# Seven block products for eight in the second matmul of a fused attention and feed-forward kernel

## The chip, the cores and the metric

The kernel runs on one core of a Trainium2 chip. The core has five engines that run side by side, each with its own instruction queue: TensorE (PE in the profile; its weight loads stand apart as PEld), VectorE (DVE), ScalarE (ACT), GpSimd (POOL) and SyncE (SP), which here only issues DMAs. Matmul results land in PSUM, which has eight banks of 128 partitions x 512 float32. The metric is the device time of one execution in microseconds (us), the median of several.

## The reference

Attention over 32 memory slots per head, then a feed-forward block whose activation is h times cos(h):

```python
a = exp(phi - max(phi, axis=2)); a = a / (sum(a, axis=2) + 1e-09)
k_m, v_m = einsum('bhsm,bhsd->bhmd', a, k), einsum('bhsm,bhsd->bhmd', a, v)
scores = matmul(q, k_m.T) / sqrt(64)
attn = softmax(scores)                 # over the 32 slots
x = matmul(attn, v_m)                  # [4608 tokens, 512]
h = x @ w_in                           # w_in  [512, 2048]
g = h * cos(h)
out = g @ w_out                        # w_out [2048, 512]
```

There are 8 batches, 8 heads, 576 tokens per batch, head width 64, all float32.

## The kernel before, in words

**Work.** The 4608 tokens are cut into 12 groups of 384 (three tiles of 128; GT). d_ff is cut into 16 tiles of 128 (NF). The main loop runs 12 x 16 = 192 iterations (i, L652); iteration i belongs to group grp = i // 16 and tile f = i % 16. v_m is folded into w_in per batch (`fold`, L442: vw), so the first product, `gemm1` (L479), multiplies the folded weights with the attention weights aT and leaves h, transposed, in one PSUM bank hp (128 x 384). Groups 1, 4, 7 and 10 straddle two batches and do this in two halves of 192 columns.

**Precision.** From group 1 on, each float32 factor is held as two float16 parts, and each product is three matmuls: high x high, high x low, low x high.

**Activation.** `act` (L498): ACT scales hp to turns and adds a quarter (L502, u), DVE rounds to int32 (L507) and subtracts (L508). `act_end` (L511): ACT takes the sine (L512), DVE multiplies with hp (L516), ACT rounds to float16 (L518), DVE forms the low part (L519). hp is free after L516.

**Second product.** `gemm2` (L524) runs four iterations later (LAG = 4). For each of the three token tiles it adds three matmuls (g high/low as weights, 512 columns of w_out as the moving side, L537) to that tile's accumulator bank; after f = 15 the banks are scaled out to SBUF (`evacuate`, L544) and stored.

**Banks.** Three for the accumulators, three for hp, two for everything else (`small_ps`).

**Beside it.** While a group runs, the attention of a later batch is made in small steps: `memory` (L214) takes the maximum of phi, its exponential, then k_m and v_m by 80 matmul records per batch over five chunks of kv into one bank psA (L247); for batches 0 to 3 the maximum comes from a transposed copy phiT by DVE and PE, for 4 to 7 by DVE and GpSimd (`maximum`, L204). `attend` (L325) makes scores, exponentials and aT. The lists `jobs` and `folds` (L641 to L649) say in which iterations the steps of a batch are emitted. In group 1 w_out and w_in are split into parts (L660 to L662).

**Order.** The program is written as one list. A scheduler places each engine's instructions in an order of its own, by priority from the place in that list and its own estimates of cost, and hands out buffers on the way; only instructions marked `keep_in_program_order` are bound. On the chip each engine then follows its list strictly and waits where an input is late.

Of the kernel before, what the change touches and what calls it, by code (L numbers as in the profile page):

```python
# [12 lines left out]
I32 = mybir.dt.int32  # L13
# [26 lines left out]
NT = 4  # L40
LAG = 4
# [3 lines left out]
def attention_then_ffn(ctx: ExitStack, tc: tile.TileContext, phi, phiT, kv, qT, w_in, w_out, eye, out):  # L45
# [5 lines left out]
    ps_acc = ctx.enter_context(tc.tile_pool(name="ps_acc", bufs=3, space=PSUM))  # L51
    ps_h = ctx.enter_context(tc.tile_pool(name="ps_h", bufs=3, space=PSUM))
    ps_s = ctx.enter_context(tc.tile_pool(name="ps_s", bufs=2, space=PSUM))

    def small_ps(name):
        return ps_s.tile([P, 512], F32, tag="ps_s", name=name)
# [15 lines left out]

    vl = const.tile([P, NP, 2, M], F16, name="vl")
    nc.vector.memset(vl, 0.0)

    loads, st = {}, {}

    def load_phi(b):
        if b < NT:
            loads["phiT", b] = t = ld.tile([P, 2, S], F32, tag="phiT", name=f"phiT_{b}", bufs=1)  # L80
            nc.sync.dma_start(out=t, in_=phiT[b].rearrange("(g p) s -> p g s", p=P))
# [5 lines left out]
    def load_kv(b):  # L87
        ts = []
        for c, (s0, n) in enumerate(TCH):
            t = ld.tile([P, H * KV], F32, tag="kv", name=f"kv_{b}_{c}", bufs=5)  # L90
            nc.sync.dma_start(out=t[:n], in_=kv[b, s0:s0 + n])
            ts.append(t)
        loads["kv", b] = ts
# [55 lines left out]

    def power_of_two(dst, src):  # L150
# [4 lines left out]
    def to_range(name, pool, tag, e):  # L155
        t = pool.tile([P, 1], F32, tag=tag, name=name)
        nc.vector.reciprocal(out=t, in_=e)
        nc.vector.tensor_scalar(out=t, in0=t, scalar1=2.0 ** 14, scalar2=None, op0=ALU.mult)
        return t

    def weight_scale(kind, name):
# [11 lines left out]
        st["s", name] = to_range(f"s_{name}", const, f"s_{name}", e)  # L173
# [30 lines left out]
    def maximum(b):  # L204
        a = loads["phi", b]
        mx = ld.tile([P, 3, HM], F32, tag="phiT", name=f"mx_{b}", bufs=1)
        nc.vector.tensor_tensor(out=mx[:, 0:2], in0=a[:, 0:2], in1=a[:, 2:4], op=ALU.max)
        nc.vector.tensor_tensor(out=mx[:, 0], in0=mx[:, 0], in1=mx[:, 1], op=ALU.max)
        nc.vector.tensor_tensor(out=mx[0:S - 512, 0], in0=mx[0:S - 512, 0], in1=a[0:S - 512, 4], op=ALU.max)
        nc.gpsimd.partition_all_reduce(mx[:, 2], mx[:, 0], channels=P, reduce_op=RED.max)  # L210
        st["top", b] = mx[:, 2]


    def memory(b):  # L214
        a = loads.pop(("phi", b))
        if b < NT:

            nmx = wk.tile([P, 2], F32, tag="nmx", name=f"nmx_{b}", bufs=1)
            nc.vector.tensor_reduce(out=nmx, in_=loads.pop(("phiT", b)), op=ALU.max, axis=AX.X)
            top = small_ps(f"top_{b}")[:, 0:HM]  # L220
            for g in range(2):
                nc.tensor.matmul(top[:, g * P:(g + 1) * P], lhsT=nmx[:, g:g + 1].broadcast_to([P, P]), rhs=ident,
                                 start=True, stop=True)
        else:
            top = st["top", b]
        yield
        if b >= NT:
            yield
            yield
        for c0, c1, n in ((0, 2, P), (2, 4, P), (4, 5, S - 512)) if b == 0 else ((0, 4, P), (4, 5, S - 512)):  # L230
            ins = nc.vector.tensor_tensor(out=a[:n, c0:c1], in0=a[:n, c0:c1],
                                          in1=top[:n].unsqueeze(1).broadcast_to([n, c1 - c0, HM]),
                                          op=ALU.subtract)
            if b >= NT:

                tc.keep_in_program_order(ins)
# [4 lines left out]
        kvs = loads.pop(("kv", b))  # L241
        psA = small_ps(f"psA_{b}")
# [496 lines left out]
```

## Time and profile before

| what | value |
|---|---|
| median of 3 runs | 720.79 us (718.35 to 721.98) |
| the profiled execution | 718.65 us, its span 716.6 us |
| TensorE clock granted | 0.99 of full speed |
| PE busy | 694.8 us, 97% |
| DVE busy | 570.0 us, 80% |
| ACT busy | 520.8 us, 73% |
| POOL busy | 14.1 us, 2% |
| groups 3 to 10 (first products start at 226.0 and 656.3 us) | 430.3 us |

The span runs from the first to the last instruction; the profiled execution's own time is 2.05 us longer. Matmuls are pipelined: one is booked from its start to its modelled end, so that neighbours overlap, and the time from one start to the next is shorter than the duration booked. Where consecutive instructions of a group are merged into a row "x9", the row's time in the chain of waits is the time that the nine took out of the span.

### The profile page before, as it was taken

To read this page: it belongs to the slowest core of one execution; us is meant where nothing else is said; L and a number is where in the kernel's file an instruction comes from. 1 tells how busy PE (TensorE), PEld (TensorE's weight loads), DVE (VectorE), ACT (ScalarE), POOL (GpSimd) and SP (SyncE) were. 2 spreads that over 40 slices of the span, in tenths; PEclk is the share of its full clock that TensorE was granted. 3 is DMA by queue.
4 is the path that set the end of the run, shared out by engine and by line. 5 is a ranking of instruction groups with operands and counts; after the bars stand their busy time and mean duration, and the time that the engine had idled before them with its cause. 6 is when DMAs were issued, how large, how long until landed. Compare 5 with 4: busy or idle time off the path is not lost.

```text
span 716.6 us, 12018 instructions
## 1 busy us (share of the span) xinstructions
PE 694.8 (97%) x4578; PEld 357.2 (50%) x4578; DVE 570.0 (80%) x1256; ACT 520.8 (73%) x965; POOL 14.1 (2%) x34
## 2 busy tenths in 40 slices
PE   7689999999999999999999999999999999999997
PEld 3244444565454445565444544666444544555553
DVE  2868999998988997679877997679776987676753
ACT  1789999899886875668757685678767785665653
POOL 0000000000000000000000100000000000000000
PEclk9799999999999999999999999999999999999999
DMA  8995881426405300152103310152100000100101
GB/s 291 381 330 168 310 291 42 121 60 188 149 7 161 111 1 1 45 167 67 45 1 123 107 49 1 45 167 68 44 1 1 22 24 1 45 1 1 45 0 45
DMA packets 31561, 66.78 MB, mean 93 GB/s; under 512 B 2192, under 2 KB 11024, under 8 KB 31504
## 3 DMA queue, kind: packets, MB, share of 16 engines
q1 hardware_dynamic: 27184, 58.15, 25.1%
q10 hardware_dynamic: 4320, 7.87, 2.9%
q8 instruction: 36, 0.59, 0.3%
q14 instruction: 21, 0.17, 0.1%
HBM read 52.38 MB, written 9.44 MB: 86 GB/s over the span
## 4 chain that ended last, share of the span: by engine, by line
PE 60%; ACT 17%; DVE 16%; DMA 4%; issue 2%; SPq 1%; POOL 0%; ACTq 0%; DVEq 0%
PE acc L537 34%; PE hp L493 18%; PE pv L432 3%; ACT u L512 2%; DVE u L516 2%; DMA phi<-in_phi 2%; DVE u L508 2%; DVE gp L519 2%; ACT u L502 2%; ACT L512 2%; DVE gp L507 1%; DMA kv<-in_kv 1%; PE sc L349 1%; ACT L237 1%; PE psA L247 1%
## 5 line engine op out<-in xcount | busy, mean ns | idle before, releaser
L537 PE MATMUL acc<-wo,gp 128*128 128x512 f16 x1584 | 371.2, 379 | 0.0
L537 PEld LDWEIGHTS <-gp 128*128 128x128 f16 x1584 | 153.4, 98 | 161.5 <-issue 2.6
L493 PE MATMUL hp<-aT,vw 128*128 128x192 f16 (+1 forms) x1440 | 202.6, 284 | 0.8 <-DVE u L516 0.4
L493 PEld LDWEIGHTS <-vw 128*128 128x128 f16 x1440 | 125.1, 98 | 82.3 <-issue 30.0
L512 ACT ACTIVATE u<-u 128x384 f32<-128x384 f32 x192 | 99.7, 522 | 86.6 <-DVE u L508 85.7
L516 DVE SCALAR_TENSOR_TENSOR u<-hp,u 128x384 f32<-128x384 f32 x176 | 96.8, 552 | 45.7 <-ACT u L512 43.4
L502 ACT ACTIVATE u<-hp,cu 128x192 f32<-128x192 f32 (+1 forms) x240 | 110.3, 491 | 18.2 <-PE hp L493 11.8
L519 DVE TENSOR_TENSOR gp<-u,gp 128x384 f16<-128x384 f32 x176 | 96.6, 551 | 29.9 <-ACT gp L518 29.3
L518 ACT CAST gp<-u 128x384 f16<-128x384 f32 x176 | 89.0, 509 | 38.7 <-DVE u L516 36.7
L508 DVE TENSOR_TENSOR u<-u,gp 128x384 f32<-128x384 f32 x192 | 105.7, 552 | 3.2
L507 DVE CAST gp<-u 128x384 int32<-128x384 f32 x192 | 67.4, 353 | 20.6 <-ACT u L502 18.9
L532 PE MATMUL acc<-wo,gp 128*128 128x512 f32 x96 | 45.5, 603 | 1.6 <-DVE gp L514 1.6
L439 DVE SCALAR_TENSOR_TENSOR vw<-pv,vw 128x512 f16<-128x512 f32 x48 | 33.0, 689 | 5.1 <-ACT vw L438 3.8
L438 ACT ACTIVATE vw<-pv 128x512 f16<-128x512 f32 x48 | 28.3, 590 | 7.4 <-PE pv L432 6.5
L484 PE MATMUL hp<-aT,vf 128*128 128x384 f32 x64 | 26.4, 546 | 4.2 <-DVE gp L514 2.0
L512 ACT ACT_TABLE_LOAD x23 | 29.5, 1283 | 0.4
L532 PEld LDWEIGHTS acc<-wo,gp 128*128 128x128 f32 x96 | 17.0, 190 | 20.7 <-issue 14.9
L247 PE MATMUL psA<-kv,phi 128*32 128x129 f32 (+1 forms) x640 | 23.5, 276 | 2.8 <-DMA kv<-in_kv 1.5
L553 ACT ACTIVATE ob<-acc,os 128x512 f32<-128x512 f32 x28 | 18.5, 682 | 8.1 <-PE acc L537 5.2
L247 PEld LDWEIGHTS psA<-kv,phi 128*32 128x32 f32 (+1 forms) x640 | 16.1, 109 | 13.3 <-issue 6.9
L484 PEld LDWEIGHTS hp<-aT,vf 128*128 128x128 f32 x64 | 12.5, 207 | 17.7 <-DVE gp L514 4.6
L349 PE MATMUL sc<-q,km 128*64 128x256 f32 (+3 forms) x192 | 20.6, 343 | 0.0
(126 smaller groups left out, 549.5 us busy)
## 6 DMA issues: line engine op xcount, KB each, us to landing
kv<-in_kv SPq DMA_DIRECT2D x32, 516.0 KB, 5.8
q<-in_qT SPq DMA_DIRECT2D x8, 1152.0 KB, 6.4
raw_out<-in_w_out SPq DMA_DIRECT2D x8, 1024.0 KB, 5.0
out<-ob ACTq DMA_DIRECT2D x30, 256.0 KB, 2.1
raw_in<-in_w_in SPq DMA_DIRECT2D x6, 1024.0 KB, 8.4
phi<-in_phi SPq DMA_DIRECT2D x8, 512.0 KB, 7.2
w_in_sb<-w_in_parts SPq DMA_DIRECT2D x12, 256.0 KB, 4.1
phiT<-in_phiT SPq DMA_DIRECT2D x4, 576.0 KB, 6.4
```

Source lines behind the costliest of these rows:

```text
L247: nc.tensor.matmul(psA[32 * j:32 * (j + 1), g * KV:(g + 1) * KV], lhsT=a[:n, c, h * M:(h + 1) * M], rhs=kvs[c][:n, h * KV:(h + 1) * KV], s ...
L484: nc.tensor.matmul(hp[:, :GT], lhsT=st["vf", q][:, g, fo * P:(fo + 1) * P], rhs=st["aTf"][:, g], start=(g == 0), stop=(g == 1))
L493: nc.tensor.matmul(hp[:, c0:c0 + n], lhsT=vw[:, wi, g, fo * P:(fo + 1) * P], rhs=aT[:, ai, g, c1:c1 + n], start=(k == 0), stop=(k == 5))
L502: ins = nc.scalar.activation(u[:, c0:c0 + n], hp[:, c0:c0 + n], AF.Copy, scale=st["cu", b] if grp else 1.0 / (2.0 * math.pi), bias=0.25)
L507: nc.vector.tensor_copy(out=ni, in_=u)
L508: nc.vector.tensor_tensor(out=u, in0=u, in1=ni, op=ALU.subtract)
L512: nc.scalar.activation(u, u, AF.Sin, scale=TWO_PI_BELOW)
L516: nc.vector.scalar_tensor_tensor(out=u, in0=hp[:, :GT], scalar=2.0 ** -17, in1=u, op0=ALU.mult, op1=ALU.mult)
L518: nc.scalar.copy(gp[:, 0], u)
L519: nc.vector.tensor_tensor(out=gp[:, 1], in0=u, in1=gp[:, 0], op=ALU.subtract)
L532: nc.tensor.matmul(accs[grp][t], lhsT=gp[:, t * P:(t + 1) * P], rhs=wo[:, f + 1], start=(f == 0), stop=(f == NF - 1))
L537: nc.tensor.matmul(accs[grp][t], lhsT=gp[:, gi, t * P:(t + 1) * P], rhs=parts[:, wi], start=(f == 0 and gi == 0 and wi == 0), stop=(f == N ...
```

## The change

In groups 3 to 10 (FIRST7, LAST7), token tiles 0 and 2 of a group and each pair of d_ff tiles (f even, f odd) form a product of 2 x 2 blocks: two token tiles x two d_ff tiles, times two d_ff tiles x two halves of 256 columns of w_out. It is made by seven block products instead of eight. Token tile 1 goes on as before (accumulator X[4]).

- **PE.** Per pair of f: six matmuls of 512 columns and 21 of 256 (`gemm2_7`), for 18 of 512. Four banks hold the seven sums of products, and a fifth tile 1.
- **Sums of g.** Per pair, four subtractions or additions of 128 x 128 float32 on GpSimd, one after the other (`act7`'s U tile, in `act_end7`).
- **Splits into float16** are made per pair, for nine blocks of 128 instead of six, in three ACT copies and three DVE subtractions (`parts7`), one iteration later.
- **Activation, groups 3 to 11.** ACT writes the scaled turns straight to int32, and one DVE instruction multiplies hp and subtracts, in place of L507 and L508; the quarter turn moves into the sine's bias.
- **Combinations of w_out** for the eight pairs are made once, by six GpSimd instructions each, and split by one ACT and one DVE instruction each (`combine`, `combine_end`), emitted at iterations 22 to 55; they are kept in SBUF that has come free.
- **Evacuation** (`evacuate7`): three ACT reads of PSUM, seven DVE additions or subtractions of 128 x 256, two ACT scalings.
- **Banks.** One tag of three ("any"), and a0, a1, a2, x0, x1 with one each. Before group 3, hp takes "any", "any", x0 in turn, and the small tiles "any", x1. From group 3 on a0 to x1 belong to the sums, and hp and all small tiles share the three of "any".
- **Buffers in SBUF.** kv has three buffers for five; chunks 3 and 4 of batches 2 to 7 are loaded in the middle of `memory`, when the first chunks are done. phiT is now used for all batches and loaded at the end of the `attend` before; `maximum` is gone. aT has two buffers for three. km and vm are cleared once, not per batch. From batch 2 on, the all-partition maximum for the scale of v_m is made by PE and DVE instead of GpSimd.
- **Lag.** LAG7 = 3 entries from group 3 on, counted after the pair has been split.

```diff
-    ps_acc = ctx.enter_context(tc.tile_pool(name="ps_acc", bufs=3, space=PSUM))
-    ps_h = ctx.enter_context(tc.tile_pool(name="ps_h", bufs=3, space=PSUM))
-    ps_s = ctx.enter_context(tc.tile_pool(name="ps_s", bufs=2, space=PSUM))
+    ps = ctx.enter_context(tc.tile_pool(name="ps", bufs=1, space=PSUM))
+    homes = {"h": ["any", "any", "x0"], "s": ["any", "x1"]}
+    turn = {"h": 0, "s": 0}
+    def bank(name, tag):
+        return ps.tile([P, 512], F32, tag=tag, name=name, bufs=3 if tag == "any" else 1)
...
+    def load_kv(b, cs=range(3)):
+        ts = loads.setdefault(("kv", b), {})
+        for c in range(5) if b < 2 else cs:
+            s0, n = TCH[c]
+            if b < 2 and c > 2:
+                t = kx[:, c - 3]
+            else:
+                t = ld.tile([P, H * KV], F32, tag="kv", name=f"kv_{b}_{c}", bufs=3)
...
+    def combine(p):
+        x = wd(p + 1).bitcast(F32) if p < 7 else ew.tile([P, 2, DM], F32, tag="U", name="x_7", bufs=2)
+        for i in range(2):
+            parts = wo_parts(2 * p + i)
+            nc.gpsimd.tensor_tensor(out=x[:, i], in0=parts[:, 0], in1=parts[:, 1], op=ALU.add)
+        a, b, c, d = (x[:, i, HW * j:HW * (j + 1)] for i in range(2) for j in range(2))
+        nc.gpsimd.tensor_tensor(out=a, in0=b, in1=a, op=ALU.subtract)
...
+    def combine_end(p, x):
+        t = wd(p)
+        nc.scalar.copy(t[:, 0].rearrange("p (c x) -> p c x", c=2), x)
+        nc.vector.tensor_tensor(out=t[:, 1].rearrange("p (c x) -> p c x", c=2), in0=x,
+                                in1=t[:, 0].rearrange("p (c x) -> p c x", c=2), op=ALU.subtract)
...
+            elif c == 2:
+                load_kv(b, (3, 4))
+                yield
+                yield
...
-        nc.gpsimd.partition_all_reduce(l3, l2, channels=P, reduce_op=RED.max)
+        if b < 2:
+            nc.gpsimd.partition_all_reduce(l3, l2, channels=P, reduce_op=RED.max)
+        else:
+            t = small_ps(f"l_{b}")[:, 0:P]
+            nc.tensor.matmul(t, lhsT=l2.broadcast_to([P, P]), rhs=ident, start=True, stop=True)
+            nc.vector.tensor_reduce(out=l3, in_=t, op=ALU.max, axis=AX.X)
...
+    def act7(grp, f, hp, pin):
+        if f % 2 == 0:
+            st["U"] = ew.tile([P, 9, TB], F32, tag="U", name=f"U_{grp}_{f}", bufs=2)
...
+            ins = nc.scalar.activation(ni[:, c0:c0 + n], hp[:, c0:c0 + n], AF.Copy, scale=st["cu", b], bias=0.25)
...
+            nc.vector.scalar_tensor_tensor(out=u[:, c0:c0 + n], in0=hp[:, c0:c0 + n], scalar=st["cu", b],
+                                           in1=ni[:, c0:c0 + n], op0=ALU.mult, op1=ALU.subtract)
...
+    def act_end7(grp, f, hp, U, u):
+        nc.scalar.activation(u, u, AF.Sin, scale=TWO_PI_BELOW, bias=quarter)
+        nc.vector.scalar_tensor_tensor(out=u, in0=hp[:, :GT], scalar=2.0 ** -19, in1=u, op0=ALU.mult, op1=ALU.mult)
...
+            for o, x, y, op in ((6, 0, 3, ALU.add), (8, 2, 0, ALU.subtract), (7, 6, 2, ALU.subtract),
+                                (0, 5, 7, ALU.subtract)):
+                nc.gpsimd.tensor_tensor(out=U[:, o], in0=U[:, x], in1=U[:, y], op=op)
...
+    def parts7(grp, f, U):
+        G = ew.tile([P, 2, 9, TB], F16, tag="G", name=f"G_{grp}_{f}", bufs=3)
+        for x, n in ((1, 5), (6, 3), (0, 1)) if grp <= LAST7 else ((0, 6),):
+            nc.scalar.copy(G[:, 0, x:x + n], U[:, x:x + n])
+            nc.vector.tensor_tensor(out=G[:, 1, x:x + n], in0=U[:, x:x + n], in1=G[:, 0, x:x + n], op=ALU.subtract)
+        return [(grp, f - 1, G), (grp, f, G)]
...
+    PARTS = ((0, 0), (0, 1), (1, 0))
+    def gemm2_7(grp, f, G):
+        if f == 0:
+            accs[grp] = [bank(f"acc7_{grp}_{i}", t) for i, t in enumerate(("a0", "a1", "a2", "x0", "x1"))]
+        X, p, last = accs[grp], f // 2, f >= NF - 2
+        w0, w1, d = wo_parts(2 * p), wo_parts(2 * p + 1), wd(p)
+        if f % 2 == 0:
+            for w, t in ((w0, 1), (w1, 4)):
+                for gi, wi in PARTS:
+                    nc.tensor.matmul(X[4], lhsT=G[:, gi, t], rhs=w[:, wi], start=(f == 0 and t == 1 and gi + wi == 0),
+                                     stop=(last and t == 4 and gi == 1))
+            todo = ((0, 0, 2, w0, 0),)
+        else:
+            todo = ((0, 1, 5, w1, 0), (3, 0, 3, d, 2), (1, 0, 6, d, 0), (1, 1, 7, d, 3), (2, 0, 8, d, 1),
+                    (2, 1, 0, w1, 1))
+        for x, half, t, w, col in todo:
+            for gi, wi in PARTS:
+                nc.tensor.matmul(X[x][:, HW * half:HW * (half + 1)], lhsT=G[:, gi, t],
+                                 rhs=w[:, wi, HW * col:HW * (col + 1)],
...
+    def evacuate7(grp):
+        X = accs[grp]
+        es = [wk.tile([P, DM], F32, tag="back", name=f"ob_{grp}_{t}", bufs=4) for t in (2, 0, 1)]
+        nc.scalar.activation(es[2], X[4], AF.Copy, scale=row_scale(grp, 1))
+        nc.scalar.copy(es[0], X[0])
+        nc.scalar.copy(es[1], X[1])
...
+    combos = {22: 0, **{33 + 3 * p: 1 + p for p in range(7)}}
...
+        if i == FIRST7 * NF:
+            homes["h"], homes["s"] = ["any"], ["any"]
+        if i in combos:
+            st["x", combos[i]] = combine(combos[i])
+        if i - 4 in combos:
+            combine_end(combos[i - 4], st.pop(("x", combos[i - 4])))
...
+        was = len(ended)
+        while len(begun) > (grp > LAST7):
+            pending.extend(act_end(*begun.pop(0)))
+        if was:
+            pending.extend(parts7(*ended.pop(0)))
+        if len(pending) > (LAG if grp < FIRST7 else LAG7):
             gemm2(*pending.pop(0))
```

More of the change, by code (lines that the diff above doesn't have):

```diff
@@ L201, in w_in_split, with wd @@
         st["w2", q] = w2
[L204 to L211, printed above, removed]
+    def wd(p):
+        if p < 2:
+            return kx.rearrange("p c x -> p (c x)")[:, p * DM * 2:(p + 1) * DM * 2].bitcast(F16).rearrange(
+                "p (w x) -> p w x", w=2)
+        if p in (4, 5):
+            return w_in_sb[:, 2 * (p - 4):2 * (p - 3), 3 * FS:].bitcast(F16)
+        key = "wd", p // 2
+        if key not in st:
+            st[key] = ld.tile([P, 2, 2, 2 * DM], F16, tag="raw1" if p < 4 else "raw2", name=f"wd_{p // 2}")
+        return st[key][:, p % 2]
```

169 lines of the change are left out of this document (105 added, 64 removed).

## Prediction

> **What bounds the kernel now.** I read the page first, then the stretches of the groups, the chain of waits, the grouped instructions, and single tiles. A difference under 0.5% (3.6 us) counts as none: about what a measurement of this kernel can tell from no change.
>
> The page's busy line, then the stretches of groups 1, 2, 3, 4, 6 and 9 and of groups 3 to 10 together (columns: stretch; its length; PE, weight loads, DVE, ACT, POOL busy; clock; DMA):
>
> ```profile
> PE 694.8 (97%) x4578; PEld 357.2 (50%) x4578; DVE 570.0 (80%) x1256; ACT 520.8 (73%) x965; POOL 14.1 (2%) x34
> ...
> 110.20:166.60 56.40, 56.22 (x348) 31.49 (x347) 55.93 (x116) 51.40 (x109) 0.31 (x1) 1.00 0.29 73
> 166.60:226.00 59.40, 58.81 (x458) 29.25 (x457) 51.11 (x123) 50.45 (x83) 0.97 (x3) 1.00 0.47 142
> 226.00:281.40 55.40, 54.97 (x336) 25.57 (x333) 48.98 (x112) 39.57 (x76) 2.04 (x4) 1.00 0.15 45
> 281.40:337.60 56.20, 56.00 (x485) 33.79 (x484) 42.96 (x101) 40.36 (x83) 2.05 (x4) 1.00 0.27 89
> 392.30:444.50 52.20, 52.20 (x304) 25.39 (x301) 46.90 (x111) 37.27 (x71) 3.05 (x4) 1.00 0.17 55
> 555.30:606.10 50.80, 50.80 (x296) 24.48 (x293) 45.36 (x108) 37.52 (x71) 0.66 (x1) 1.00 0.04 17
> 226.00:656.30 430.30, 428.97 (x3024) 224.30 (x3021) 342.29 (x771) 301.58 (x590) 9.54 (x16) 1.00 0.15 49
> ```
>
> In the 430.3 us that the change touches, PE lacks work for 1.3 us. DVE is second, 80% on the mean but 90% in groups 6 and 9 (46.90 of 52.20), and PE does not stop there: DVE at 90% is no limit yet. In group 1 it ran at 99%. So a saving on PE is a saving in time, as long as DVE, ACT and the banks keep up.
>
> **The change on PE.** Is a matmul of half the columns half the time, though it loads weights as often? Two rows of the chain of waits, back to back: 6 matmuls of 512 columns, then 12 of 192 columns (group 4):
>
> ```profile
> 299.18 1.94 PE acc L537 x9
> 301.12 1.00 PE hp L493 x12
> ```
>
> Nine of 512 take 1.94 us, 216 ns each; twelve of 192 take 1.00, 83 ns each, and each has a weight load of its own, which stays hidden. On the line through both, 256 columns cost 83 + 64 x 133/320 = 110 ns. A pair of f falls from 18 x 216 = 3.89 us to 6 x 216 + 21 x 110 = 3.61, by 0.28 to 0.29. There are 8 groups x 8 pairs: **-18.6 us**, 2.3 in each group.
>
> PE also gains work. The prices of all that follows:
>
> ```profile
> L508 DVE TENSOR_TENSOR u<-u,gp 128x384 f32<-128x384 f32 x192 | 105.7, 552 | 3.2
> L512 ACT ACTIVATE u<-u 128x384 f32<-128x384 f32 x192 | 99.7, 522 | 86.6 <-DVE u L508 85.7
> L516 DVE SCALAR_TENSOR_TENSOR u<-hp,u 128x384 f32<-128x384 f32 x176 | 96.8, 552 | 45.7 <-ACT u L512 43.4
> L519 DVE TENSOR_TENSOR gp<-u,gp 128x384 f16<-128x384 f32 x176 | 96.6, 551 | 29.9 <-ACT gp L518 29.3
> L518 ACT CAST gp<-u 128x384 f16<-128x384 f32 x176 | 89.0, 509 | 38.7 <-DVE u L516 36.7
> L507 DVE CAST gp<-u 128x384 int32<-128x384 f32 x192 | 67.4, 353 | 20.6 <-ACT u L502 18.9
> L502 ACT ACTIVATE u<-hp,cu 128x384 f32<-128x384 f32 x112 | 63.8, 576 | 12.6 <-PE hp L493 8.9 <-ACT ob L553 1.7 <-DVE gp L507 0.4
> L378 DVE SCALAR_TENSOR_TENSOR aT<-back,aT 128x512 f16<-128x512 f32 x14 | 9.5, 678 | 0.0
> L377 ACT ACTIVATE aT<-back 128x512 f16<-128x512 f32 x14 | 8.8, 626 | 1.5 <-DVE back L375 1.1
> L237 ACT ACTIVATE phi<-phi 128x1024 f32<-128x1024 f32 x7 | 7.4, 1057 | 0.1
> L231 DVE TENSOR_TENSOR phi<-phi,mx 128x1024 f32<-128x1024 f32 x4 | 4.9, 1218 | 0.0
> L287 POOL PARTITION_ALL_REDUCE l<-l x8 | 4.0, 495 | 348.5 <-DVE l L285 348.5
> L222 PE MATMUL top<-ident,nmx 128*128 128x128 f32 x16 | 2.5, 281 | 0.5 <-DVE nmx L219 0.5
> L271 POOL MEMSET vm<- 128x256 f32 x8 | 2.5, 319 | 80.1 <-PE pv L426 38.7 <-DVE vl L318 38.5 <-DVE om L565 2.9
> L377 ACT ACTIVATE aT<-back 128x128 f16<-128x128 f32 x7 | 2.1, 297 | 0.2 <-DVE back L375 0.2
> L378 DVE SCALAR_TENSOR_TENSOR aT<-back,aT 128x128 f16<-128x128 f32 x7 | 2.0, 284 | 0.2 <-ACT aT L377 0.2
> L208 DVE TENSOR_TENSOR mx<-mx 128x256 f32<-128x256 f32 x4 | 1.6, 412 | 0.0
> ```
>
> The maximum of phi on PE (L222) cost 2.5 us for four batches and now comes for four more: +2.5. The maximum for the scale of v_m is half of it, in six batches: +1.9. Together **+4.4 us**, in groups 2 to 8. Both are durations with overlap, so ceilings; the floor is nothing, and the range uses it. If all else hides, 718.65 - 18.6 + 4.4 is 14.2 us less.
>
> **DVE.** Gone per f are L507, L508 and L519: 353 + 552 + 551 = 1456 ns, 23.3 us per group. New per f is one instruction like L516: 552 ns, 8.8 us per group; in straddling groups two of 192 columns, about 355 each (L378 gives (678-284)/384 = 1.03 ns a column): 11.4. New per pair are three splits of 640, 384 and 128 columns: 551 + 256 x 1.03 = 814, 551 and 284, 1.65 us, or 13.2 per group. The evacuation adds 7 x 412 (L208) = 2.9. Net per group: +1.6, or +4.2 where it straddles. The split of each w_out combination costs 1.22 (L231, same size): four fall into group 2 and three into group 3. What `maximum` gives back, phiT's reduction takes; I count it zero.
>
> So DVE needs, against PE's need: group 3, 48.98 + 1.6 + 3.7 = 54.2 against about 53.1; group 6, 48.5 against 49.9; group 9, 47.0 against 48.5; group 4, 47.2 against some 55. In group 3 DVE becomes the bound: I take 55.0, so 1.9 us of the gain is lost there. In 6 and 9 it works at 97%, more than the 90% that was free: I charge 1 us each. Group 2 goes to 51.11 + 4.9 = 56.0 of 59.4, ACT to 50.45 + 4 x 1.06 (L237) = 54.7; I charge 1 us.
>
> **ACT.** The three copies per pair cost 297 + 509 + 728 (slope (626-297)/384 from L377) = 1.53 us against 2 x 509 before: +4.1 us per group, and the two scalings of the evacuation some 1.3. Group 6 goes to 42.7 of 50: no bound, since the chain turns, subtraction, sine, product is one instruction shorter than before (L507 is gone).
>
> **GpSimd.** No row shows a two-input instruction there. Nearest are L271, 0.32 us for 256 columns written and none read, so some 0.2 for 128 as floor, and the all-reduce with 0.50 as ceiling. I take 0.3, nearer to the memset, which works per element: four sums per pair are 1.2 us of some 5.5; the combinations (48 instructions, at twice the columns or more some 0.6 to 1.2 us each) have four iterations each, some 13 us. `parts7` stands an iteration behind its sums. That cover holds for an iteration, 2.6 us per pair; beyond it ACT's second copy waits with the next iteration's turns queued behind it.
>
> The Trainium skill has a rule against this (SBUF — State Buffer, "Who interferes with whom"): a DVE instruction with two SBUF inputs and a GpSimd instruction that reads SBUF exclude each other, the later blocking wholly. No row here can show it, as GpSimd hardly reads; rival 2 prices it.
>
> **Banks and kv.** hp and all small tiles now share three banks for five. An hp's least life is 1.0 (gemm1) + 576 + 552 + 522 + 552 = 3.2 us, PE's iteration about 2.6, so two banks pass an hp in time if its life stays under 5.2. A row that speaks against it, with the tiles psA and kv:
>
> ```profile
> 404.15 1.15 PE L493 MATMUL hp<-aT,vw 128*128 128x384 f16 x6
> ...
> 407.56 1.15 PE L493 MATMUL hp<-aT,vw 128*128 128x384 f16 x6
> ...
> 413.78 1.02 DVE L516 SCALAR_TENSOR_TENSOR u<-hp,u 128x384 f32<-128x384 f32 x2
> ...
> L247 PE MATMUL psA<-kv,phi x320: 270/273/298, 305.0 to 555.1; 128*32 128x129 f32 x128, 64*32 64x129 f32 x32
> L261 DVE TENSOR_SCALAR X<-psA,den x8: 341/348/351, 312.6 to 557.5; 128x128 f32<-128x128 f32 x8
> ...
> DMA to landing us min/median/max: 3.5/6.1/13.2
> ```
>
> During an attention step two hp live until 414.3 and 414.8, 10.2 and 7.2 us, because DVE and ACT do other work first. psA held a bank from 305.0 to 312.6 in the first batch of this stretch, and will hold it for a kv load more (6.1 median). PE can bridge this with the second product, of which three to five tiles (1.8 us each) lie ready; so the forecast charges nothing, with rival 3 as the other end. On SP's queue the two late kv loads wait for the first chunks' matmuls, with the next batch's phi and kv behind them; these are due a whole attention step later, so I charge nothing. phiT, now loaded when an attention step ends, must land (about 6 us by the kv row, for a similar size) before the next maximum: only batch 3 follows at once, and PE has first and second products meanwhile.
>
> The new evacuation costs PE nothing: X[4] ends at f = 14, X[0] early in f = 15, and the rest are needed two first products later.
>
> The tail is unchanged: group 11 keeps the old product and its last six tiles.
>
> **Sum.** -18.6 + 4.4 + 1.9 + 2 + 1 = -9.3 against the profiled 718.65: 709.3. The median is 2.1 above that execution, so the forecast is **711.5 us**.
>
> **Rivals.**
>
> 1. *All of it hides.* DVE in group 3 hands work to its neighbours, and 97% is no more of a limit than group 1's 99%: 720.8 - 14.2 = 706.5. For it: PE's idle time of 1.3 us in 430. Against: group 1 was DVE's, not PE's.
>
> 2. *DVE is blocked by GpSimd's sums and becomes the bound.* 24 splits per group read two SBUF operands; if two in three wait for one sum of 0.3, that is 4.8 us of DVE per group. Groups 3, 6 and 9 then take 59.0, 53.3 and 51.8, against 55.4, 52.2 and 50.8: +5.7 instead of a gain. The other five keep 5 x 2.3 - 4.0 = 7.5, group 2 loses 1: net -0.8, 720. By the skill's rule that is about what comes out if sums and splits fall together often. It decides once DVE waits over some 1.5 us per group. Against: sums are emitted one iteration ahead of their splits.
>
> 3. *Banks (slower).* While psA waits for its late kv chunks, some 14 us per batch, two banks serve hp; with lives of 7.2 they pass one per 3.6 us, 4 iterations instead of 5.4, a loss of 3.6. Scores and the exponentials' table loads cost about 2.5 more. Five batches (3 to 7) make 30 us: 720.8 - 14.2 + 30 = 736. It decides from lives over 5.2 us, with the stored second products used up. For it: the 10.2 above. Against: DVE and ACT may be handed another order where banks are few.
>
> That 256 columns cost more than half (weight loads as the limit) I give little: the 83 ns row.
>
> **How the numbers follow.** Forecast 0.38, rival 1 0.25, rival 2 0.20, rival 3 0.14, rest 0.03. Low is 702, rival 1 with PE's new work at its floor (720.8 - 18.6); high is 728, past rival 2 and into the first half of rival 3. Faster by over 3.6 us are the forecast and rival 1 with a little of 2: 0.65. Within: most of rival 2 and a mild 3: 0.18. Slower: the rest, 0.17.
>
> **What would show it.** PE: 1344 matmuls of 256 columns at starts 110 ns apart; groups 5, 8 and 10 shorter by about 2 us with PE never idle. DVE: about 54 us busy in group 3, at 97% in 6 and 9. GpSimd: 256 sums near 0.3 us; if splits on DVE come out longer than 814, 551 and 284, rival 2 is at work. PE's weight loads of the first product waiting for DVE's last use of hp would be rival 3. The forecast is wrong if 256 columns cost over 125 ns, or PE idles over 10 us in groups 3 to 10.

## The result

The changed kernel takes 758.6 us (median of four runs, 756.87 to 759.87) against 720.1 for the kernel before on the same chip: 1.053 times as long, 95% interval 1.050 to 1.057. The forecast was 711.5, faster; the time lies far outside its range. Its profiled execution has a span of 757.0 us.

The profile after: the page's busy line, then the stretches of the changed kernel (columns as in the prediction). The seven are: groups 1, 2, 3, 4, 6, 9, each from the first product of its first tile to that of the next group, and groups 3 to 10 together.

```profile
PE 690.2 (91%) x5182; PEld 419.2 (55%) x5182; DVE 631.5 (83%) x1283; ACT 567.6 (75%) x1039; POOL 202.9 (27%) x313
...
116.00:175.70 59.70, 56.28 (x350) 31.83 (x349) 59.53 (x101) 47.23 (x99) 13.41 (x11) 1.00 0.27 67
175.70:253.40 77.70, 64.94 (x458) 32.22 (x457) 70.77 (x136) 55.79 (x93) 33.31 (x32) 0.91 0.39 118
253.40:310.50 57.10, 53.37 (x375) 29.43 (x372) 51.76 (x103) 44.40 (x82) 24.33 (x35) 1.00 0.16 54
310.50:367.60 57.10, 54.64 (x564) 41.45 (x562) 49.55 (x119) 46.63 (x94) 15.83 (x31) 1.00 0.28 88
426.90:478.70 51.80, 48.91 (x362) 31.55 (x361) 46.85 (x91) 39.45 (x75) 18.27 (x32) 1.00 0.15 51
595.90:647.20 51.30, 48.95 (x362) 31.56 (x361) 45.88 (x89) 39.49 (x75) 18.94 (x32) 1.00 0.04 16
253.40:695.60 442.20, 418.46 (x3599) 281.50 (x3596) 380.35 (x802) 339.13 (x664) 151.13 (x258) 1.00 0.17 55
```

Two things are to be seen. First, most of the loss lies where the seven products are not yet used: groups 0 to 2 end at 253.4 us instead of 226.0 (+27.4), and group 2 alone grew from 59.4 to 77.7. DVE is busy 130.3 of the 137.4 us of groups 1 and 2, 95%, and GpSimd works there for 47 us, almost all of it on the combinations of w_out. Second, in groups 3 to 10 PE's busy time fell from 429.0 to 418.5, but its idle time rose from 1.3 to 23.7 us, so that the stretch grew from 430.3 to 442.2.

Part of group 2's growth shows on PE as a lower clock: 0.91 of full speed in the table, 1.00 before, and 64.9 us of busy time for the same 458 records that took 58.8. Twice, from 182.7 and from 203.2 us, the granted clock stood at half for 6.8 us; the first time it fell while PE waited 5.5 us for ACT's exponential. The first of these stretches:

```profile
182.70:189.50 6.80, 4.80 (x53) 2.90 (x54) 5.79 (x11) 6.71 (x9) 3.38 (x2) 0.50 0.68 154
```

How much of the 18 us the lower clock adds, beside a DVE that is busy for 91% of the group, was not taken apart.

PE's price was as forecast. A row of the chain of waits, 18 matmuls of 256 columns back to back:

```profile
305.42 1.96 PE acc L643 x18
```

1.96 us for 18 is 109 ns each; the forecast had 110. So the loss is not in the price of these matmuls. It shows in the groups of instructions: GpSimd's sums, and DVE's splits of 640, 384 and 128 columns.

```profile
L582 POOL TENSOR_TENSOR U<-U 128x128 f32<-128x128 f32 x256 | 147.5, 579 | 333.4 <-DVE U L575 307.6 <-DVE l L328 8.3 <-DVE ev L179 7.7
L592 DVE TENSOR_TENSOR G<-U,G 128x640 f16<-128x640 f32 x64 | 57.2, 893 | 12.2 <-ACT G L591 11.8
L592 DVE TENSOR_TENSOR G<-U,G 128x384 f16<-128x384 f32 x64 | 41.1, 642 | 2.7 <-ACT G L591 2.7
L592 DVE TENSOR_TENSOR G<-U,G 128x128 f16<-128x128 f32 x64 | 22.6, 354 | 0.0
```

The splits were forecast at 814, 551 and 284 ns. Read with the start and end of every instruction in the trace, the 14, 28 and 34 of them that met no GpSimd instruction, or for under 40 ns, took 816, 547 and 279 in the median; the others averaged 914, 716 and 437.

The timeline of group 2, DVE and then GpSimd in the same 9 us, shows how one such instruction grows:

```profile
190.88 0.56 DVE L616 SCALAR_TENSOR_TENSOR u<-hp,u 128x384 f32<-128x384 f32 x1 [1.28 <-ACT u L612]
191.35 1.29 DVE L605 CAST gp<-u 128x384 int32<-128x384 f32 x1
192.68 0.96 DVE L606 TENSOR_TENSOR u<-u,gp 128x384 f32<-128x384 f32 x1
193.57 1.50 DVE L619 TENSOR_TENSOR gp<-u,gp 128x384 f16<-128x384 f32 x1
...
198.47 1.01 DVE L616 SCALAR_TENSOR_TENSOR u<-hp,u 128x384 f32<-128x384 f32 x2
```

```profile
190.16 2.26 POOL L248 TENSOR_TENSOR w_in_sb<-wo 128x512 f32<-128x512 f16 x2 [1.59 <-DMA w_in_sb<-w_in_parts]
192.38 0.84 POOL L250 TENSOR_TENSOR w_in_sb<-w_in_sb 128x256 f32<-128x256 f32 x1
193.19 1.46 POOL L248 TENSOR_TENSOR w_in_sb<-wo 128x512 f32<-128x512 f16 x1
```

The cast and the two subtractions, 0.35, 0.55 and 0.55 us in the kernel before, take 1.29, 0.96 and 1.50; each ends 0.2 to 0.4 us after a GpSimd instruction has ended. The product L616, whose first operand lies in PSUM, keeps its 0.56 and, twice over, 1.01.

### The profile page after: what moved, and what is told of

Its sections match the earlier page's. It is cut to its first block, busy times and chain, and to the rows that moved or that the text cites. A ratio compares the mean times of both kernels' runs of the same rounds, so it can differ in the third digit from the quotient of the medians.

```text
span 757.0 us, 13553 instructions
## 1 busy us (share of the span) xinstructions
PE 690.2 (91%) x5182; PEld 419.2 (55%) x5182; DVE 631.5 (83%) x1283; ACT 567.6 (75%) x1039; POOL 202.9 (27%) x313
## 4 chain that ended last, share of the span: by engine, by line
DVE 32%; PE 30%; ACT 23%; issue 5%; DMA 4%; POOL 4%; SPq 1%; ACTq 0%; DVEq 0%; POOLq 0%
PE hp L543 9%; PE acc L643 7%; DVE G L592 6%; PE acc L688 4%; PE acc L635 4%; DVE U L569 3%; ACT U L565 3%; DVE U L575 3%; POOL U L582 3%; ACT G L591 3%; DVE ob L665 2%; ACT U L574 2%; DMA kv<-in_kv 2%; DVE u L606 2%; PE pv L482 2%
## 5 line engine op out<-in xcount | busy, mean ns | idle before, releaser
L582 POOL TENSOR_TENSOR U<-U 128x128 f32<-128x128 f32 x256 | 147.5, 579 | 333.4 <-DVE U L575 307.6
L643 PEld LDWEIGHTS <-G 128*128 128x128 f16 x1344 | 130.6, 98 | 41.3 <-issue 9.6
L592 DVE TENSOR_TENSOR G<-U,G 128x640 f16<-128x640 f32 (+3 forms) x200 | 122.7, 643 | 20.7 <-ACT G L591 20.1
L591 ACT CAST G<-U 128x640 f16<-128x640 f32 (+3 forms) x200 | 102.4, 523 | 40.1 <-POOL U L582 26.8
L565 ACT ACTIVATE U<-hp,cu 128x384 int32<-128x384 f32 (+1 forms) x192 | 89.8, 494 | 28.3 <-PE hp L543 20.3
L569 DVE SCALAR_TENSOR_TENSOR U<-hp,cu,U 128x384 f32<-128x384 f32 (+1 forms) x192 | 93.3, 508 | 16.7 <-ACT U L565 15.7
L635 PE MATMUL acc<-wo,G 128*128 128x512 f16 x384 | 95.5, 379 | 0.1
L643 PE MATMUL acc<-wo,G 128*128 128x256 f16 x576 | 94.6, 273 | 0.1
L688 PE MATMUL acc<-wo,gp 128*128 128x512 f16 x288 | 71.2, 387 | 6.4 <-DVE gp L619 2.1
L635 PEld LDWEIGHTS <-G 128*128 128x128 f16 x384 | 36.6, 98 | 36.7 <-issue 1.6
L688 PEld LDWEIGHTS <-gp 128*128 128x128 f16 x288 | 27.4, 99 | 38.1 <-issue 7.6
L688 PE MATMUL acc<-wo,G 128*128 128x512 f16 x144 | 32.9, 379 | 0.0
```

Of the source, the lines that this page charges most:

```text
L565: ins = nc.scalar.activation(ni[:, c0:c0 + n], hp[:, c0:c0 + n], AF.Copy, scale=st["cu", b], bias=0.25)
L569: nc.vector.scalar_tensor_tensor(out=u[:, c0:c0 + n], in0=hp[:, c0:c0 + n], scalar=st["cu", b], in1=ni[:, c0:c0 + n], op0=ALU.mult, op1=AL ...
L582: nc.gpsimd.tensor_tensor(out=U[:, o], in0=U[:, x], in1=U[:, y], op=op)
L591: nc.scalar.copy(G[:, 0, x:x + n], U[:, x:x + n])
L592: nc.vector.tensor_tensor(out=G[:, 1, x:x + n], in0=U[:, x:x + n], in1=G[:, 0, x:x + n], op=ALU.subtract)
L635: nc.tensor.matmul(X[4], lhsT=G[:, gi, t], rhs=w[:, wi], start=(f == 0 and t == 1 and gi + wi == 0), stop=(last and t == 4 and gi == 1))
```

## The experiments

**Theory:** GpSimd's reads of SBUF hold up DVE instructions that need two operands from SBUF; DVE thereby becomes the bound, in groups 1 and 2 by the combinations, in groups 3 to 10 by the sums ("port theory"). **Rivals:** too few banks for hp and the small tiles ("bank theory"); the added DVE and ACT work as such; and the kv loads, which come late ("late-load theory").

### Sums of g left out

```diff
-            for o, x, y, op in ((6, 0, 3, ALU.add), (8, 2, 0, ALU.subtract), (7, 6, 2, ALU.subtract),
-                                (0, 5, 7, ALU.subtract)):
-                nc.gpsimd.tensor_tensor(out=U[:, o], in0=U[:, x], in1=U[:, y], op=op)
...
+            y = x - 3 if x == 6 else x
+            nc.scalar.copy(G[:, 0, x:x + n], U[:, y:y + n])
```

> The four GpSimd sums per pair are left out; the splits read unsummed blocks in their place, so ACT, DVE and PE keep every instruction. Port theory (a DVE instruction with two SBUF inputs is held up while GpSimd reads SBUF): in the changed kernel the splits took 893, 642 and 354 ns, against 816, 547 and 279 where no GpSimd instruction overlapped them, 16 us over 64 pairs, and ACT waited 27 us for sums. Then the splits come down to about 816, 547 and 279, groups 3 to 10 lose 12 to 20 of their 442 us, and the whole takes 739 to 747. Bank theory (hp and the small tiles have too few banks): the splits may get shorter, but groups 3 to 10 keep their stalls, and the whole stays over 753. Groups 0 to 2 do not change by either.

743.2 us, 15.4 less than the changed kernel. The splits in its profile, and groups 3 to 10:

```profile
L588 DVE TENSOR_TENSOR G<-U,G 128x640 f16<-128x640 f32 x64 | 52.4, 818 | 11.5 <-ACT G L587 11.0
L588 DVE TENSOR_TENSOR G<-U,G 128x384 f16<-128x384 f32 x64 | 35.1, 548 | 0.0
L588 DVE TENSOR_TENSOR G<-U,G 128x128 f16<-128x128 f32 x64 | 17.8, 279 | 1.4 <-ACT G L587 1.3
```

```profile
255.00:682.70 427.70, 415.82 (x3598) 281.44 (x3595) 363.19 (x805) 337.81 (x667) 6.10 (x6) 1.00 0.17 56
```

The splits are back at their own length, DVE has 17.2 us less to do, and the stretch loses 14.5, as the port theory had it. PE's idle time halves, to 11.9; the other half has another cause.

The edit takes away more than the hold-up, though: ACT's waits for the sums themselves go too. And the sign that the prediction had named for too few banks, PE waiting for DVE's last use of hp, did appear in the changed kernel. The first two lines are waits of the changed kernel (the second in groups 3 to 10), the last is the same wait of PE without the sums:

```profile
ACT G L591 <- POOL U L582: 26.8, 59, 1.7
PE hp L543 <- DVE U L575: 10.1, 14, 1.4
...
PE hp L543 <- DVE U L575: 3.1, 6, 0.7
```

With the banks unchanged, 7.0 of the 10.1 us go with the sums: DVE reached its last use of hp late, and the bank came free late.

### Combinations of w_out left out

```diff
-            st["x", combos[i]] = combine(combos[i])
-        if i - 4 in combos:
-            combine_end(combos[i - 4], st.pop(("x", combos[i - 4])))
+            nc.gpsimd.memset(wd(combos[i]).bitcast(F32), 0.0)
```

> The combinations of w_out are left out: one GpSimd memset each stands for the six GpSimd instructions, the ACT copy and the DVE subtraction. Port theory: groups 1 and 2 lose the 10.6 us of DVE subtractions and the some 14 us by which DVE instructions with two SBUF inputs grew there; 137.4 us becomes 113 to 120, the whole 734 to 742. If only the added DVE work counts and not the blocking: about 127, the whole 748. Bank theory (the turn-taking banks of groups 0 to 2 are the cause): 132 or more, the whole over 753. Groups 3 to 10 change by less than 5 us, since three combinations end in group 3.

740.1 us, 18.5 less. Groups 1 and 2 take 124.1 instead of 137.4, group 3 54.0 instead of 57.1; that is a smaller part in groups 1 and 2 than expected, and the whole within what was expected.

### Both left out

> Both left out: sums of g and combinations of w_out. GpSimd then reads SBUF hardly at all. Port theory: the two savings add up, 718 to 728, and what remains over 706 is DVE and ACT work that was priced too low, and the banks. Bank theory: over 745.

724.3 us, 34.3 less; 15.4 and 18.5 make 33.9, so the two causes add up. Almost without GpSimd reads the kernel is still 0.7% slower than the one before (1.007, interval 1.004 to 1.010), and 18 us above the 706.5 of rival 1.

### Only GpSimd's part of the combinations left out

The two runs above took DVE's and ACT's work away with GpSimd's. Here that work stays.

```diff
-        for i in range(2):
-            parts = wo_parts(2 * p + i)
-            nc.gpsimd.tensor_tensor(out=x[:, i], in0=parts[:, 0], in1=parts[:, 1], op=ALU.add)
...
-        nc.gpsimd.tensor_tensor(out=c, in0=d, in1=c, op=ALU.subtract)
+        nc.gpsimd.memset(x, 0.0)
```

> The changed kernel, with the six GpSimd instructions of each w_out combination replaced by one memset; the ACT copy and the DVE subtraction of each stay. It leaves the combinations' values out. This splits the 18.5 us that the combinations cost in all (758.6 to 740.1). Port theory: most of it is blocking, since DVE instructions with two SBUF inputs grew by some 14 us in groups 1 and 2 and the subtractions there are 10.6: groups 1 and 2 go from 137.4 us to 125 to 130, the whole to 747 to 751. If the added DVE and ACT work is the cost: 133 or more, the whole over 754.

740.8 us, within 0.7 of the run without any combination, and below the 747 to 751 expected. So eight ACT copies and eight DVE subtractions cost nothing that can be told, and the whole 18 us is GpSimd's. Groups 1 and 2 in this run:

```profile
115.20:170.80 55.60, 55.60 (x350) 31.82 (x349) 55.49 (x112) 50.45 (x105) 2.06 (x2) 1.00 0.30 72
170.80:237.40 66.60, 60.78 (x464) 30.83 (x462) 59.28 (x134) 53.62 (x91) 3.84 (x4) 0.97 0.49 144
```

They take 122.2 us instead of 137.4, 15.2 less, and DVE is busy 114.8 instead of 130.3, 15.5 less, though a few more of its instructions fall into these groups. That is what a DVE held up by GpSimd would give. Two smaller things go along with it and were not separated: ACT's waits for the combinations, 4.3 us in the changed kernel, and the lower clock (0.97 here in group 2, 0.91 there).

### GpSimd as a bystander in the kernel before

Two kernels test the mechanism by itself, with neither the seven products nor their banks. The first adds, per pair of f, four subtractions on GpSimd that read SBUF; the second one subtraction of a single column and eight memsets.

```diff
+        if 3 <= grp <= 10 and f % 2:
+            for x in (u[:, 0:112], idle, idle, idle):
+                nc.gpsimd.tensor_tensor(out=idle, in0=x, in1=idle, op=ALU.subtract)
```

> The kernel before, with GpSimd work added as a bystander: per pair of f in groups 3 to 10 four subtractions of 112 columns, whose result nobody uses. Port theory: DVE's subtractions with two SBUF inputs (L508, L519, 552 and 551 ns) and the cast (L507, 353) grow by up to half a GpSimd instruction on the mean, where they meet one; the product that reads PSUM (L516) stays at 552. DVE has 20% to spare in these groups, so the whole grows by 2 to 10 us. Without such blocking: nothing grows, 720.

728.9 us against 719.8 (1.013, interval 1.010 to 1.016). The loss is spread over groups 4 to 9, with 1.2 to 1.8 us each. Its rows, of which L508, L516 and L507 are those of the kernel before and L522 is its L519:

```profile
L508 DVE TENSOR_TENSOR u<-u,gp 128x384 f32<-128x384 f32 x192 | 109.4, 571 | 5.4
...
L522 DVE TENSOR_TENSOR gp<-u,gp 128x384 f16<-128x384 f32 x176 | 102.1, 583 | 28.5 <-ACT gp L521 27.9
L516 DVE SCALAR_TENSOR_TENSOR u<-hp,u 128x384 f32<-128x384 f32 x176 | 96.7, 552 | 44.6 <-ACT u L512 43.5
L507 DVE CAST gp<-u 128x384 int32<-128x384 f32 x192 | 74.7, 391 | 18.3 <-ACT u L502 16.9
```

```diff
+            nc.gpsimd.tensor_tensor(out=idle[:, 0:1], in0=u[:, 0:1], in1=idle[:, 0:1], op=ALU.subtract)
+            for _ in range(8):
+                nc.gpsimd.memset(idle, 0.0)
```

> The kernel before, with a bystander that only writes: per pair of f in groups 3 to 10 one subtraction of one column and eight memsets of 112 columns, about as long on GpSimd as the four subtractions. If it is GpSimd's reads that block a second SBUF input, L508 and L519 stay at 552 and 551 and the whole at 719 to 722. If any GpSimd activity does, they grow as in the run with subtractions. The Trainium skill (SBUF — State Buffer, Who interferes with whom) has it that an instruction that only writes does not contend with two SBUF inputs, but does with DVE's two-port modes; then the cast L507 alone might grow.

728.6 us, which was not expected, but with these rows (L523 is L519 of the kernel before; the last is ACT's scaling of hp to turns):

```profile
L508 DVE TENSOR_TENSOR u<-u,gp 128x384 f32<-128x384 f32 x192 | 105.7, 552 | 5.9
...
L516 DVE SCALAR_TENSOR_TENSOR u<-hp,u 128x384 f32<-128x384 f32 x176 | 96.8, 552 | 49.2 <-ACT u L512 46.7
L523 DVE TENSOR_TENSOR gp<-u,gp 128x384 f16<-128x384 f32 x176 | 96.4, 551 | 31.9 <-ACT gp L522 31.2
L507 DVE CAST gp<-u 128x384 int32<-128x384 f32 x192 | 68.4, 357 | 28.5 <-ACT u L502 26.9
...
L502 ACT ACTIVATE u<-hp,cu 128x384 f32<-128x384 f32 x112 | 63.8, 576 | 25.3 <-PE hp L493 10.7 <-POOL idle L518 9.2 <-POOL idle L520 1.8
```

With GpSimd reading, the instructions with two SBUF operands grew from 552 and 551 to 571 and 583, the cast from 353 to 391, and the one with an operand in PSUM stayed at 552. With GpSimd only writing, the subtractions kept their length and the cast gained 4 ns. So it is the reading that holds up the subtractions. The memset kernel's 9 us have another origin: in its profiled execution, with 733.4 us the slowest of four, groups 5 and 8 take 62.5 and 61.6 us instead of 54.7 and 54.5, and the other groups are as before. ACT waits there for the bystander (L518), which stands in GpSimd's queue and reads the buffer that ACT wants to write, PE stands still, and its clock falls to half for 6.8 us in each of the two groups. In the run with subtractions ACT never waits for GpSimd. The bystander was not as idle as I meant it.

By the Trainium skill (SBUF — State Buffer, "Who interferes with whom"), a DVE instruction with two SBUF inputs excludes a GpSimd instruction that reads SBUF, but not one that only writes; both halves agree with these two runs (583 and 551 ns). The same section lets DVE's two-port modes, which a cast can enter, contend with any GpSimd instruction, the later of the two blocking: 391 with reads agrees. With writes alone it is the memsets that lose: they take 192 ns where they meet no cast, and 283 in the median where they meet one.

### Sums on DVE

```diff
-                nc.gpsimd.tensor_tensor(out=U[:, o], in0=U[:, x], in1=U[:, y], op=op)
+                nc.vector.tensor_tensor(out=U[:, o], in0=U[:, x], in1=U[:, y], op=op)
```

> The changed kernel, with the four sums per pair on DVE instead of GpSimd. Port theory: the blocking of the splits (16 us over 64 pairs) and ACT's 27 us of waits for GpSimd go, but DVE gets 4 x 279 ns per pair, 71 us, and needs some 435 of the 442 us of groups 3 to 10: DVE becomes the bound there, the whole 762 to 785. If the place of the sums were the fault rather than DVE's load, it would be faster than 758.6.

750.7 us: faster than the changed kernel by 7.9, where I had expected it slower. Groups 3 to 10:

```profile
254.00:690.20 436.20, 421.00 (x3599) 280.19 (x3596) 408.70 (x1057) 342.65 (x670) 6.09 (x6) 1.00 0.17 55
```

DVE's 256 sums took 284 ns each, 72 us, and it is busy 409 of 436 us; still the stretch is 6 us shorter than with the sums on GpSimd. I had taken DVE's 94 to 98% for a hard bound, and the sums' detour over GpSimd (579 ns each, four in a row, with ACT waiting for them) for the lesser evil.

Group 6 shows it best, first without sums, then with the sums on DVE:

```profile
424.20:473.30 49.10, 48.45 (x360) 31.55 (x360) 45.49 (x91) 39.38 (x76) 0.00 (x0) 1.00 0.15 53
427.10:476.00 48.90, 46.38 (x338) 28.91 (x337) 48.35 (x118) 41.13 (x76) 0.00 (x0) 1.00 0.16 54
```

On DVE, busy for 99% of the group, the sums cost no time there (over groups 3 to 10 they cost 8.5 us, 436.2 against 427.7); on GpSimd, with DVE busy for 90%, the group took 51.8. So that part of the theory fails: in groups 3 to 10 the sums do not make DVE the bound. They lengthen the way from one instruction to the next, by holding up DVE's splits and by letting ACT wait (26.8 us in the changed kernel, 4.9 here). How the 15.4 us divide between the two was not tried.

### kv loaded early

This run and most of those after it start from the one without sums and combinations (724.3), in which only banks, loads and instruction prices are left.

In that run, SyncE's queue, and PE's first instruction after the wait in group 2:

```profile
172.54 1.45 SPq L227 DMA_DIRECT2D w_in_sb<-w_in_parts  x1
174.62 3.20 SPq L118 DMA_DIRECT2D kv<-in_kv  x3
```

```profile
181.41 0.87 PE L286 MATMUL psA<-kv,phi 128*32 128x129 f32 x12 [2.51 <-DMA kv<-in_kv]
```

The late kv chunks are issued at 174.6, behind four copies of w_in, and PE stands still for 2.5 us until they land. With all five chunks loaded at once (the 8 KB per partition come from leaving out kx):

```diff
-        for c in range(5) if b < 2 else cs:
...
-                t = ld.tile([P, H * KV], F32, tag="kv", name=f"kv_{b}_{c}", bufs=3)
+        for c, (s0, n) in enumerate(TCH):
+            t = ld.tile([P, H * KV], F32, tag="kv", name=f"kv_{b}_{c}", bufs=5)
...
-                load_kv(b, (3, 4))
```

> As the run with neither sums nor combinations (724.3 us), and in addition kv as before: five buffers, all five chunks of a batch loaded at once; the kx buffer is gone, and its two pairs read another pair's cleared combination. Late-load theory: in that run PE stood still 6 us before psA in group 2, behind kv chunks issued at 174.6 and 224.0; group 2 falls from 67.9 us to 60 to 62, and 1 us falls away in each of four or five later batches: 712 to 718. Bank theory: the stalls only move to other waits, group 2 stays over 65, the whole over 721.

716.1 us, 8.2 less; group 2 falls from 68.0 to 61.9 and groups 3 to 10 from 424.2 to 421.4. The late-load theory holds. This is also the first kernel that beats the one before, by 3.7 us (0.995, interval 0.993 to 0.997), though with the sums and combinations left out it is a bound and not a kernel.

### Banks

> As the run before this one, and in addition the banks of groups 0 to 2 as before the change (three for hp, two for the small tiles). If the turn-taking banks cost time there, groups 0 and 1 lose the 3 to 5 us by which they grew (114.4 against 110.2, group 1 55.6 against 56.4), and the whole is 3 to 5 us under that run; if the loads in another order cost it, the difference is under 2. What then remains over 706 belongs to groups 3 to 10: the banks there, and ACT and DVE instructions priced too low.

```diff
-    homes = {"h": ["any", "any", "x0"], "s": ["any", "x1"]}
+    homes = {"h": ["any"], "s": ["x0", "x1"]}
...
-        psA = bank(f"psA_{b}", "x1") if b < 3 else small_ps(f"psA_{b}")
+        psA = small_ps(f"psA_{b}")
```

718.0 us, not less than 716.1: the turn-taking banks of groups 0 to 2 are not where those groups lost their time.

> The kernel before with one part of the change alone: from group 3 on hp and all small tiles share three banks, and two banks stay empty (but for two accumulators of group 11, as before). Port theory: within 4 us of 720, as the tiles in use exceeded three in 9% of that time. Bank theory: PE's first product waits for DVE's last use of hp; 735 or more. In between, the share of each is read from the difference.

```diff
     def small_ps(name):
+        if shared:
+            return ps_h.tile([P, 512], F32, tag="ps_h", name=name)
...
+        if i == 3 * NF:
+            shared.append(1)
```

728.5 us against 719.2 (1.013, interval 1.009 to 1.017): in the kernel before, three shared banks cost 9 us, most of it in groups 4, 6 and 7.

> As the run without sums and combinations and with kv as before (716.1 us), and in addition a fourth bank: tile 1's product is added into X[0], so that x1 is free in groups 3 to 10 for small tiles, in turn with the three shared ones. The output mixes two tiles; PE's instructions are the same in number and size. Bank theory: PE stood still 10.4 us in groups 3 to 10 of that run against 2.5 before, and the kernel before lost 9 us to three shared banks; so 3 to 8 us fall away: 708 to 713. If the stalls are those of evacuation and of ACT's and DVE's longer work: 714 to 718.

```diff
-            accs[grp] = [bank(f"acc7_{grp}_{i}", t) for i, t in enumerate(("a0", "a1", "a2", "x0", "x1"))]
+            accs[grp] = [bank(f"acc7_{grp}_{i}", t) for i, t in enumerate(("a0", "a1", "a2", "x0"))]
+            accs[grp].append(accs[grp][0])
...
-            homes["h"], homes["s"] = ["any"], ["any"]
+            homes["h"], homes["s"] = ["any"], ["any", "x1"]
```

717.1 us, no change from 716.1. Its waits of PE in groups 3 to 10:

```profile
PE acc L625 <- ACT ob L648: 4.5, 5, 1.6
PE hp L536 <- DVE U L568: 2.0, 7, 0.4
```

With four banks PE waits 2.0 us for one to come free, and 4.5 for the evacuation; that the shared X[0] delays it is likely, but not shown. In the run with three banks the same waits were 3.2 us (hp and psA behind DVE's last use of hp) and 2.4 us. So the fourth bank saved about 1 us and cost 2 elsewhere, and even without that cost it could have saved 3 at most. Banks were dearer in the kernel before, whose hp passes through one more instruction; whether that is the reason was not tested. (The idle times of 10.4 and 2.5 us in that expectation are worked out from the matmuls' starts; by the busy columns they are 7.6 and 1.3.)

### The quarter turn left out

```diff
-        nc.scalar.activation(u, u, AF.Sin, scale=TWO_PI_BELOW, bias=quarter)
+        nc.scalar.activation(u, u, AF.Sin, scale=TWO_PI_BELOW)
```

> The changed kernel without the quarter turn in the sine of groups 3 to 11, so that it makes a sine where the reference has a cosine. The sine with a bias from a tile took 615 ns against 522 before. I expect 522 again, 13 us less ACT work over 144 instructions. ACT is not the bound (339 of 442 us in groups 3 to 10), so the whole stays between 754 and 759; if the length of the chain that holds a bank counts, each hp is free 0.09 us earlier, and the whole falls to 748 to 753.

The sine took 522 ns again, as expected, but the whole took 767.1, 8.5 more than with the quarter turn. Groups 6 and 9 went from 51.8 and 51.3 us to 55.5 and 57.5, and both GpSimd (20 us in each, against 18 and 19) and DVE (48.8 and 47.9, against 46.9 and 45.9) were busy for longer there on the same work. The edit made the scheduler lay out the instructions anew, and presumably the new order met GpSimd's sums at worse places. What it was in that order was not tried. Any single difference of under some 8 us among kernels with GpSimd sums may hold such luck, the 7.9 us of the run with the sums on DVE too; the sums' and combinations' 15 and 18 us do not rest on one such difference, since they were found twice each, alone and together.

## Why the prediction was wrong, point by point

- **PE's saving: right.** 109 ns against 110. With the GpSimd work and the late loads out of the way, PE's busy time in groups 3 to 10 is 413.8 us against 429.0 before, 15.1 less; the forecast had 14.2 net, with the added maxima at their ceiling. (The row of nine matmuls of 512 columns is called "6 matmuls" once in the prediction; the sum goes by nine.)
- **The term that failed: the combinations of w_out.** The prediction gave GpSimd's 48 instructions a cover of "four iterations each, some 13 us" and charged group 2 with 1 us, for DVE's splits. They nearly fit into their cover (ACT waited 4.3 us for them in groups 1 and 2), and their price, 54 us for the 48, was within the range given. But while they read, DVE's casts and subtractions waited. DVE was at 86% of group 2 already and went to 91% of a group 18 us longer. Measured: 18 us, all of it GpSimd's part, and in groups 1 and 2 as much as DVE's busy time grew by.
- **The sums: the hold-up was rival 2's, its way into the time was not.** "If two in three wait for one sum of 0.3" gave 4.8 us of DVE per group and 720, or 8.5 over the forecast. Measured, 116 of the 192 splits met a GpSimd instruction, a sum took 457 ns in the median and 579 on the mean, and DVE lost about 2 us per group. Yet leaving the sums out saved 15.4, since the loss did not come from a full DVE but from what waited behind it and behind the sums. The rival also forgot that the same rule held for the combinations, whose instructions of 512 columns are three to four times as long (1.36 us and more) and which fall into groups 1 and 2, where DVE had been busy for 99% and 86%. It had 0.20 and would have come out as slower, not as no change.
- **DVE at 97% as a limit: not seen.** The forecast charged 1 us each in groups 6 and 9. In the run that reached 716.1 they took 49.1 and 48.8 us, 3.1 and 2.0 less than before, with DVE at 93% and 90%; with the sums on DVE they took 48.9 and 49.0 at 99%. On this point rival 1 was right.
- **"On SP's queue ... I charge nothing": wrong, 8.2 us.** The late chunks are issued behind other copies and PE has to wait, above all in group 2, where 6.1 of the 8.2 us were lost.
- **The prices of ACT and DVE: too low by small sums.** The sine took 615 instead of 522, since its bias is a tile, and the new product L569 610 instead of 552. Its scale is a tile too, which is the likely reason: in the kernel before, L439 took 744 with such a scale and 689 without. Over 16 tiles that is 1.5 and 0.9 us per group. ACT was no bound, as forecast.
- **Banks: the forecast's zero holds to within 3 us.** That was tested without sums and combinations. In the changed kernel PE did wait 10.1 us for hp, rival 3's sign, but 7.0 of them went with the sums. Rival 3's 736 was the nearest of the four, 23 us short and by another mechanism. Of the prediction's own signs, PE's idle time of over 10 us (23.7) and the longer splits came true.
- **What was left open.** With all of this taken out, 716.1 remains, against 706.5 for rival 1. Groups 3 to 10 hold some 6 us of idle PE above the kernel before, and groups 0 and 2 are 4.2 and 2.5 us longer (114.4 and 61.9 against 110.2 and 59.4), where aT, phiT and the order of the loads are different too. These were not taken apart.

The sum of what was shown, from 758.6: sums and combinations 34.3, late kv loads 8.2, which leaves 716.1, 3.7 under the 719.8 of the kernel before. So of the 38.5 us, the sums and combinations on GpSimd account for almost 90%, and the loads for the rest of the loss and the gain that it ate. That GpSimd's reads hold up DVE is shown by the bystander; that this hold-up, and not the waits for GpSimd's results, is most of the 34.3 is well supported for the combinations and open for the sums. No version with the sums and combinations in it came near the kernel before; the best of them, with the sums on DVE, takes 750.7.

## What to carry to other kernels

Work moved to an idle GpSimd is not free for DVE: before moving it, count the DVE instructions in that stretch that read two operands from SBUF, or cast, and add to each up to the length of a GpSimd instruction that it may meet. A one-off preparation can cost more than what it prepares saves: here 47 us of GpSimd work in groups 1 and 2 lengthened them by 15 us, as much as the seven products save on PE in all of groups 3 to 10. And a second engine's share of busy time is a poor measure of what more work on it costs: in groups 6 and 9 DVE went from 93% and 90% to 99% at a loss of 0.3 us at most, while the same sums on an idle engine, four in a row with others waiting for them, cost 2 to 3 us in each.

## What the runs showed of the hardware

- A DVE cast from float32 to int32, with one SBUF operand, is held up by GpSimd's reads as much as an instruction with two: 353 to 391 ns on the mean with the bystander, 1.29 us in the worst case shown above.
- A per-partition operand costs time on both engines: on ACT the sine went from 522 to 615 ns with a bias from a tile, on DVE the fused multiply and subtract L439 takes 744 with a scale from a tile and 689 with an immediate, for the same 128 x 512 in the kernel before. For ACT, the Trainium skill (ScalarE: Activation LUTs, "What ACT_TABLE_LOAD costs") has about 93 ns for each such operand, which agrees with the 93 seen here.
- In this kernel, DVE with 72 us more of its own work (94% busy) was 7.9 us faster than with the same sums on a GpSimd that is idle three quarters of the time.
- The granted TensorE clock fell to half while PE idled, and stayed there after its work came back: in the changed kernel PE idled from 179.2 to 184.7 us and the clock was at half from 182.7 to 189.5; in groups 5 and 8 of the memset kernel PE idled for 3.9 and 3.7 us, with 6.8 us of half clock each. In groups 1 to 10 of the kernel before PE never idled for over 0.5 us at a stretch, and the clock stayed at 1.00.
